# Attention feeding routed experts on one core: banks, places and order of the score maxima and of three small products

## The chip, the cores and the metric

One core of a Trainium2 chip runs one program. The metric is device time in microseconds of one execution; each kernel is given by the median of several runs. Engines: TensorE (PE; its weight loads PEld), VectorE (DVE), ScalarE (ACT), GpSimd (POOL), SyncE (SP, which issues DMAs). TensorE writes PSUM, which has eight banks of 512 fp32 columns for each of 128 partitions; VectorE and ScalarE read them.

## The reference

```
q_pool = q.reshape(8, 8, 576, 2, 64).mean(axis=3)        # 8 batches, 8 heads, 1152 keys
scores = q_pool @ k.T / 8
attn   = softmax(scores, axis=-1)                         # its maximum subtracted
x      = (attn @ v) as 4608 tokens x 512
logits = x @ w_gate + modality_bias[modality_id]          # 8 experts
e      = argmax(logits); g = softmax(logits)[e]
out    = g * (relu(x @ w1[e]) @ w2[e])                    # 512 -> 1024 -> 512
```

All inputs are fp32.

## The kernel before

**Tiles and stages.** Two batches of one head make a *pair*; there are 32 pairs. For each pair the kernel finds for every query a bound on its scores (the *row*: minus the maximum over all keys of the high fp16 part), computes the scores (L978, L979, fp16 with high and low parts, into one of three banks `psc`), takes the exponential on ScalarE (L980, 432 columns each), splits off the exponentials' low part `Pl` (L961 on ScalarE, L963 on VectorE) and multiplies with the values (L1038 to L1040) into bank X0 for the first head of the pair and X1 for the second. `evac` (L1056 to L1061) divides by the sums. The experts follow after all pairs.

**Order of the work.** Every engine's queue is written out by hand. The loop at the end of `attention` goes through 18 *steps* for each pair (`NSTEP`), and strings of letters (`ORD`) say what each step issues: `s` a score part, `v` the value products of 128 queries (three of them), `E` an event, `J` a piece of routing, `F` what was put off with `later`. `ends(t)` then issues what is due at the end of a step. Times such as `T_SQ = -19` count steps from the start of the pair that the work is for, so work for a pair is done during the two pairs ahead of it. Step numbers below are those within a pair, 0 to 17.

**Five shared banks.** Besides the three `psc` banks there are M0 and M1 (one tile `pm` of two banks), M2, X0 and X1. A product into a bank waits for whoever read it before.

- For pairs 0 to 2 `first_max` and `maxpass` compute score maxima block by block, through M0, M1 and M2 in turn.
- From pair 3 on, six *events* for each pair do this: block 4 (step 13), event 0 (16), event 1 (1), the rest (4), event 2 (7) and event 3 (10). Events 0 to 3 issue four products of 512 columns (L921): in the order M0, M2, M1, X0 or X1. VectorE takes the maxima (L903): M0 and M1 in one instruction of 1024 columns, then M2, then X0 or X1. After event 3 the maxima are combined (`m`, L843), and three steps later, at the end of step 13, TensorE transposes them into M2 (L847), VectorE makes the row `mr` (L856) and SP sends it to the score operand B2.
- Other products use `some()`, which is M2 while events run: the routing product (L289) in step 9 of every second pair, whose result VectorE adds to the logits (L295) in step 10; the scales' product (L787, `power`) at the end of step 2, read by `half` (L793) and two more small instructions (L795); the placing products of the router (L353, L355), allowed only in steps 2, 3, 13, 14 and 15.

**The scales.** `square` (step 17) sums the squares of a pair's values on ScalarE (L781), `power` and `scales` make powers of two of it, GpSimd copies one (`both`, L802) and scales the values (VH, L823, steps 3 and 4). GpSimd's first VH (`values` with part 1) and its sum of the queries (`split_q`, L688) wait for VectorE's latest L963 (`hold`).

```
ORD = ('NvJMvsvMsvXF', 'JvvsEMvvXFvv', 'vFvvsJvXv')
later_end(PD if p else 0, lambda: scales(p, pt))
```

Of the kernel before, what the change touches and what calls it, by code (L numbers as in the profile page):

```python
# [9 lines left out]
F32 = mybir.dt.float32  # L10
# [8 lines left out]
PSUM = bass.MemoryType.PSUM  # L19
# [3 lines left out]
P = 128  # L23
# [15 lines left out]
NSTEP = 2 * NKC  # L39
# [38 lines left out]
V1 = (9, 11, (14, 15), 18, (18, 19))  # L78
LOWS0 = (((0, 1152, 'A', 2), (1152, 1728, 'D', 3)),)
LAG0 = 7  # L80
T_SQ = -19
T_POW = -16
T_VH = (-14, -15)
T_VL = (-11, -2)
T_VS = -12
# [73 lines left out]
T_MX2 = -23  # L159
BY_HEADS = 3  # L160
EVENTS = (("block4", -23), (0, -20), (1, -17), ("rest", -14), (2, -11), (3, -8))
T_ROW = 3
M0, M1, X0, M2, X1 = range(5)
FIN = 0
FD = 0
# [446 lines left out]
def attention(tc, ctx, att, ident, npairs, xpool, on_two, on_split, on_scale, jobs, side, set_pm, started, ahead, hip):  # L612
# [7 lines left out]
    pvl = ctx.enter_context(tc.tile_pool(name="avl", bufs=3))  # L620
    sm = ctx.enter_context(tc.tile_pool(name="asm", bufs=3))
    ps_sc = ctx.enter_context(tc.tile_pool(name="pssc", bufs=3, space=PSUM))
    ps_all = ctx.enter_context(tc.tile_pool(name="psall", bufs=1, space=PSUM))
    m01 = ps_all.tile([P, 2, 512], F32, name="pm")
    m2, x0, x1 = (ps_all.tile([P, 512], F32, name=n) for n in ("pm2", "xp0", "xp1"))
    banks = [m01[:, 0], m01[:, 1], x0, m2, x1]
    turns3 = itertools.cycle((M0, M1, M2))
    now, flushed = [0], [-1]
    by_events = lambda: BY_HEADS * NSTEP + EVENTS[0][1] <= now[0] < (npairs - 1) * NSTEP
    bank = lambda: banks[next(turns3)]  # L630
    some = lambda: banks[M2] if by_events() else bank()
    set_pm(some, lambda: by_events() and now[0] % NSTEP not in (2, 3, 13, 14, 15))

    ones = const.tile([P, 1], BF16, name="ones")
# [204 lines left out]
    def row(p, mp, u0, u1):  # L839

        n = u1 - u0
        m9 = sm.tile([P, 9], F32, name="m9")
        nc.vector.tensor_reduce(m9[:, 0:n], mp[:, u0:u1], op=ALU.max, axis=AX.X, negate=True)  # L843

        def finish():
            pt = some() if p else banks[X1 if u0 else X0]
            nc.tensor.transpose(pt[0:n, 0:P], m9[:, 0:n], ident)  # L847
            if now[0] > NSTEP:
                later_end(FD, lambda: put(pt))
            else:  # L850
                put(pt)

        def put(pt):
            mr = sm.tile([9, P], F16, name="mr", bufs=1)
            made.add((p, f"row{u1}"))
            nc.vector.tensor_scalar(mr[0:n], pt[0:n, 0:P], 1.0 / ROW, 16.0 * math.log(PSC) / ROW, op0=ALU.mult, op1=ALU.add)  # L856
            done = st[p]["row"] = (nc.sync if p or u0 else nc.scalar).dma_start(out=B2[p % 2][D:D + 1, 2 * S + u0 * P:2 * S + u1 * P], in_=mr[0:n])
            if turns:
                with tc.issue_after(done.ins):
                    while turns:  # L860
                        turns.pop(0)()
        return finish
# [32 lines left out]
    def event(p, what):  # L895

        s = st[p]
        need(p, "qh", "hi0", "hi1")
        if "mp" not in s:
            s["mp"] = sm.tile([P, 9, 3], F32, name="mp")  # L900
        mp, hi = s["mp"], s["hi"]
        queries = lambda j, i: s["qh"][half[j], j * D + i * P:j * D + (i + 1) * P]
        most = lambda o, x: nc.vector.tensor_reduce(o, x, op=ALU.max, axis=AX.X)  # L903
        mixed = QB[p % 2][:, 4]
        if what == "block4":
            for t in range(2):
                nc.tensor.matmul(banks[M0 + t], mixed, hi[:, t * 512:(t + 1) * 512], start=True, stop=True)
            most(mp[:, 4, 0:2], m01)
        elif what == "rest":
            nc.tensor.matmul(banks[M1][:, 0:P], mixed, hi[:, 1024:S], start=True, stop=True, skip_group_check=True)  # L910
            for i in range(4):
                for j, b in ((0, M0), (1, M2)):
                    nc.tensor.matmul(banks[b][:, i * P:(i + 1) * P], queries(j, i), hi[half[j], 1024:S], start=True, stop=True, skip_group_check=True)
            by_block = lambda x: x.rearrange("p (u k) -> p u k", k=P)
            most(mp[:, 5:9, 2], by_block(m2))
            most(mp[:, 0:5, 2], by_block(m01.rearrange("p b n -> p (b n)")[:, 0:5 * P]))
        else:
            second = (M2, X0 if what < 2 else X1)
            for t in range(2):
                for j, to in ((0, M0 + t), (1, second[t])):  # L920
                    nc.tensor.matmul(banks[to], queries(j, what), hi[half[j], t * 512:(t + 1) * 512], start=True, stop=True)  # L921
            most(mp[:, what, 0:2], m01)
            for t in range(2):
                most(mp[:, 5 + what, t:t + 1], banks[second[t]])
        if what == EVENTS[-1][0]:
            later_end(T_ROW, row(p, mp, 0, 9))

# [147 lines left out]
    mxq, pvq, scq = [], [], []  # L1075
# [20 lines left out]
    def advance(q, n):  # L1096
        for _ in range(n):
            while q and next(q[0], DONE) is DONE:
                q.pop(0)
# [82 lines left out]
    for p in range(npairs):  # L1182
        b = NSTEP * p
# [54 lines left out]
    for t in range(NSTEP * npairs):  # L1238
        p, c18 = divmod(t, NSTEP)
        now[0] = t  # L1240
        if jobs and c18 in (JOBS if p < npairs - 1 else JOBS_LAST):
            running.append(jobs.pop(0))
        for a in ORD[t % len(ORD)]:
            if a == "J":
                running[:] = [g for g in running if next(g, DONE) is not DONE]
# [509 lines left out]
```

## Time and profile before

| | us |
|---|---|
| median of 3 runs (1200.7 to 1202.91) | 1201.41 |
| the profiled execution, its own time | 1202.61 |
| its span, first to last instruction | 1200.8 |
| TensorE busy | 1109.9 |
| VectorE busy | 982.9 |
| ScalarE busy | 893.7 |
| GpSimd busy | 438.0 |

The rows come from that one profiled execution. Times count from the start of its span. "Idle before" is the time that an engine stood ahead of an instruction, with the instruction that ended the wait behind the arrow. Instructions of an engine overlap a little at their ends, so the start of the next one can lie before the end of the last. PEclk is the granted share of TensorE's clock: 1.00 is 2.4 GHz, 0.50 is 1.2 GHz.

### The profile page before, as it was taken

What the parts mean: (1) busy time and instruction counts of PE and PEld (TensorE: products, weight loads), DVE (VectorE), ACT (ScalarE), POOL (GpSimd) and SP (SyncE); (2) the same over time, 40 slices, a digit from 0 to 9 for tenths busy, and PEclk for the clock granted to TensorE, in tenths of its full rate; (3) what the DMA queues carried; (4) which work ended last, traced back from release to release, by engine and by line L of the source; (5) the groups of instructions that cost most, each with busy time, mean ns of one, the idle gap of its engine ahead of it and who ended that gap; (6) DMA issues with size and microseconds to landing.
All of it is one profiled execution on the core that took longest, in us unless ns stands there. A gap on an engine that the chain in (4) does not pass through costs nothing.

```text
span 1200.8 us, 36624 instructions
## 1 busy us (share of the span) xinstructions
PE 1109.9 (92%) x15060; PEld 787.3 (66%) x15060; DVE 982.9 (82%) x1730; ACT 893.7 (74%) x1403; POOL 438.0 (36%) x469
## 2 busy tenths in 40 slices
PE   7888989989889899898999989999999999999997
PEld 3566666666656666665666766677667676766665
DVE  6778979989878898987989999987798767575665
ACT  5778878878868788886888888887665656565654
POOL 7644434453434435443334544312322221212111
PEclk9999989999989999998999999999999999999999
DMA  7757667776676767866668676559999999999993
GB/s 220 201 119 167 162 154 165 180 173 164 147 153 170 174 163 164 184 148 157 164 147 184 175 164 132 126 163 284 289 269 271 316 272 280 269 290 279 280 275 116
DMA packets 179696, 237.41 MB, mean 198 GB/s; under 512 B 96479, under 2 KB 127215, under 8 KB 179520
## 3 DMA queue, kind: packets, MB, share of 16 engines
q1 hardware_dynamic: 169254, 206.65, 65.2%
q0 software_dynamic: 10256, 28.33, 11.4%
q8 instruction: 120, 1.97, 0.7%
q14 instruction: 56, 0.46, 0.1%
q10 hardware_dynamic: 10, 0.00, 0.0%
HBM read 163.22 MB, written 18.99 MB: 152 GB/s over the span
## 4 chain that ended last, share of the span: by engine, by line
PE 63%; DVE 33%; issue 2%; DMA 1%; ACT 1%; SPq 0%; POOL 0%; POOLq 0%
DVE mp L903 18%; PE psc L979 7%; PE psc L978 6%; PE ph L1411 5%; PE ph L1410 5%; PE ph L1412 5%; PE po L1519 5%; PE po L1517 5%; PE po L1518 5%; DVE Pl L963 5%; PE xp L1038 4%; PE xp L1040 3%; PE xp L1039 3%; PE pm L921 3%; DVE x L1007 2%; DVE x L1061 2%
## 5 line engine op out<-in xcount | busy, mean ns | idle before, releaser
L980 ACT ACTIVATE Pe<-psc 128x432 int32<-128x432 f32 x768 | 384.6, 527 | 135.8 <-PE psc L979 119.0
L1038 PE MATMUL xp<-VH,Pe 128*128 128x65 f16 x2880 | 354.6, 196 | 0.0
L1038 PEld LDWEIGHTS <-Pe 128*128 128x128 f16 x2880 | 270.1, 98 | 128.6 <-issue 85.0
L1040 PE MATMUL xp<-VS,Pl 128*128 128x65 f16 x2880 | 351.6, 194 | 0.8 <-DVE Pl L963 0.8
L1039 PE MATMUL xp<-vl,Pe 128*128 128x64 f16 x2880 | 350.9, 193 | 0.0
L903 DVE TENSOR_REDUCE mp<-pm 128x2 f32<-128x1024 f32 (+3 forms) x319 | 287.8, 940 | 67.0 <-PE xp L921 39.1
L979 PE MATMUL psc<-B 65*128 65x432 f16 (+2 forms) x1152 | 310.8, 293 | 1.9 <-DMA B<-mr 1.9
L978 PE MATMUL psc<-B 128*128 128x432 f16 (+2 forms) x1152 | 310.8, 292 | 0.2 <-ACT Pe L980 0.2
L1039 PEld LDWEIGHTS <-Pe 128*128 128x128 f16 x2880 | 269.6, 99 | 46.4 <-issue 2.4
L1040 PEld LDWEIGHTS <-Pl 128*128 128x128 f16 x2880 | 267.9, 98 | 1.2 <-DVE Pl L963 1.2
L961 ACT ACTIVATE Pl<-Pe 128x1152 f16<-128x1152 uint16 x186 | 216.5, 1164 | 5.9
L1411 PE MATMUL ph<-xpart,w1h 128*128 128x256 f16 x544 | 148.3, 273 | 0.0
L1412 PE MATMUL ph<-xpart,w1l 128*128 128x256 f16 x544 | 148.3, 273 | 0.0
L1410 PE MATMUL ph<-xpart,w1h 128*128 128x256 f16 x544 | 148.3, 273 | 0.0
L963 DVE TENSOR_SCALAR Pl<-Pe 128x576 f16<-128x576 uint16 (+1 forms) x198 | 125.9, 637 | 4.5 <-ACT Pe L980 3.5
L978 PEld LDWEIGHTS <-B 128*128 128x128 f16 x1152 | 113.5, 99 | 10.6 <-issue 4.8
L688 POOL TENSOR_TENSOR rawq<-rawq 128x576 f32<-128x576 f32 x31 | 43.8, 1414 | 210.0 <-DVE Pl L963 210.0
L979 PEld LDWEIGHTS <-B 65*128 65x128 f16 x1152 | 114.8, 100 | 7.8 <-issue 0.5
L1416 DVE SCALAR_TENSOR_TENSOR hl<-ph,hh 128x512 f16<-128x512 f32 x72 | 49.7, 690 | 73.2 <-ACT hh L1415 68.3
L1517 PE MATMUL po<-w2h,hh 128*128 128x512 f16 x288 | 109.2, 379 | 0.0
L1518 PE MATMUL po<-w2l,hh 128*128 128x512 f16 x288 | 109.2, 379 | 0.0
L1519 PE MATMUL po<-w2h,hl 128*128 128x512 f16 x288 | 109.2, 379 | 0.0
(300 smaller groups left out, 1927.3 us busy)
## 6 DMA issues: line engine op xcount, KB each, us to landing
w2r<-in_w_dram SPq DMA_DIRECT2D x76, 512.0 KB
w1r<-in_w_dram SPq DMA_DIRECT2D x72, 512.0 KB
rawv<-in_att_dram SPq DMA_DIRECT2D x32, 576.0 KB
B<-hi SPq DMA_DIRECT2D x128, 144.0 KB
rawq<-in_att_dram SPq DMA_DIRECT2D x31, 576.0 KB
rawk<-in_att_dram SPq DMA_DIRECT2D x31, 576.0 KB
B<-qh SPq DMA_DIRECT2D x128, 72.0 KB
B<-lo SPq DMA_DIRECT2D x64, 144.0 KB
```

Of the source, the lines that this page charges most:

```text
L903: most = lambda o, x: nc.vector.tensor_reduce(o, x, op=ALU.max, axis=AX.X)
L961: nc.scalar.activation(low, rest, AF.Copy, scale=LOW)
L963: fast[0] = (nc.vector if eng == 'D' else nc.gpsimd).tensor_single_scalar(low, rest, LOW, op=ALU.mult)
L978: nc.tensor.matmul(o, b1[:, ks], b1[:, qs], start=True, stop=False, skip_group_check=True)
L979: nc.tensor.matmul(o, b2[:, ks], b2[:, qs], start=False, stop=True, skip_group_check=True)
L980: nc.scalar.activation(Pe[:, D + x0:D + x1], pt, AF.Exp, scale=1.0 / 16)
L1038: nc.tensor.matmul(out, Ph[:, qs], vh[:, c, j, 0:D + 1], start=c == 0 and g == 0, stop=False, skip_group_check=True)
L1039: nc.tensor.matmul(out[:, 0:D], Ph[:, qs], vl[:, c, j], start=False, stop=False, skip_group_check=True)
L1040: nc.tensor.matmul(out, Pl[:, qs], vs[:, c, j, 0:D + 1], start=False, stop=c == NKC - 1, skip_group_check=True)
L1410: nc.tensor.matmul(o, hi[:, c, fs], xh[:, :, c], start=c == 0, stop=False)
L1411: nc.tensor.matmul(o, hi[:, c, fs], xl[:, :, c], start=False, stop=False)
L1412: nc.tensor.matmul(o, lo[:, c, fs], xh[:, :, c], start=False, stop=c == 3)
```

## The change

It does five things. M0, M1 and M2 are three tiles of one bank each until step 13 of pair 1; `join_banks` then issues one more piece of the maxima that are due, closes their pool, and takes a tile of two banks for M0 and M1 and one for M2. In events 0 to 3 the maxima of M2 and of X0 or X1 come ahead of those of M0 and M1. The square goes from step 17 to step 16 and the scales' product from the end of step 2 to the end of step 0 (pairs 2 and later). The row's transposing product goes from the end of step 13 to the end of step 12 (`T_ROW`) and keeps M2. Products that `some()` serves in steps 13, 14 and 15 go to X0.

```
-T_SQ = -19
-T_POW = -16
+T_SQ = -20
+T_POW = -18
...
-T_ROW = 3
+T_ROW = 2
...
-    ps_all = ctx.enter_context(tc.tile_pool(name="psall", bufs=1, space=PSUM))
-    m01 = ps_all.tile([P, 2, 512], F32, name="pm")
-    m2, x0, x1 = (ps_all.tile([P, 512], F32, name=n) for n in ("pm2", "xp0", "xp1"))
-    banks = [m01[:, 0], m01[:, 1], x0, m2, x1]
+    ps_x = ctx.enter_context(tc.tile_pool(name="psx", bufs=1, space=PSUM))
+    banks = {X0: ps_x.tile([P, 512], F32, name="xp0"), X1: ps_x.tile([P, 512], F32, name="xp1")}
+    singles = ExitStack()
+    ps_one = singles.enter_context(tc.tile_pool(name="psone", bufs=1, space=PSUM))
+    for i in (M0, M1, M2):
+        banks[i] = ps_one.tile([P, 512], F32, name=f"pm{i}")
     turns3 = itertools.cycle((M0, M1, M2))
+
+    def join_banks():
+        advance(mxq, 1)
+        assert not mxq
+        singles.close()
+        ps_two = ctx.enter_context(tc.tile_pool(name="pstwo", bufs=1, space=PSUM))
+        two, banks[M2] = ps_two.tile([P, 2, 512], F32, name="pm01"), ps_two.tile([P, 512], F32, name="pm2")
+        banks["both"], banks[M0], banks[M1] = two, two[:, 0], two[:, 1]
...
-    some = lambda: banks[M2] if by_events() else bank()
+    some = lambda: banks[X0 if now[0] % NSTEP in (13, 14, 15) else M2] if by_events() else bank()
+    apart = lambda: banks[M2] if by_events() else bank()
...
-            pt = some() if p else banks[X1 if u0 else X0]
+            pt = apart() if p else banks[X1 if u0 else X0]
...
-            most(mp[:, what, 0:2], m01)
             for t in range(2):
                 most(mp[:, 5 + what, t:t + 1], banks[second[t]])
+            most(mp[:, what, 0:2], banks["both"])
...
+        if t == BY_HEADS * NSTEP + EVENTS[0][1]:
+            join_banks()
```

## Rows read from the trace of the kernel before

**Rows 1.** Busy time of each engine in two stages (us from the span's start): length, then busy us and number of instructions of PE, PEld, DVE, ACT and POOL, granted clock, DMA share, GB/s.

```profile
14.00:75.00 61.00, 48.94 (x633) 32.71 (x630) 46.12 (x92) 43.82 (x71) 39.25 (x67) 0.97 0.62 168
75.00:790.00 715.00, 648.35 (x11145) 471.91 (x11146) 633.36 (x1179) 592.13 (x982) 302.38 (x299) 0.97 0.69 161
```

**Rows 2.** Who waited for whom, TensorE alone, 75 to 790 us: us in total, times, longest us.

```profile
PE pm L289 <- DVE mp L903: 23.5, 14, 2.0
PE pm L787 <- DVE mp L903: 18.7, 28, 1.2
PE pm L921 <- DVE mr L856: 8.3, 12, 0.7
PE pm L353 <- DVE mr L856: 7.5, 2, 3.7
...
PE psc L979 <- DMA B<-mr: 1.9, 1, 1.9
```

**Rows 3.** Busy time in short stretches, columns as in rows 1; the granted clock is the third number from the end.

```profile
117.60:121.00 3.40, 3.40 (x34) 1.99 (x32) 1.41 (x4) 2.50 (x4) 3.06 (x3) 0.50 0.59 174
155.20:158.50 3.30, 3.30 (x40) 2.05 (x38) 1.09 (x1) 2.29 (x4) 0.46 (x1) 0.50 0.69 143
...
346.30:353.10 6.80, 6.33 (x63) 4.09 (x63) 1.28 (x6) 2.62 (x5) 0.32 (x1) 0.50 0.62 150
...
612.60:615.90 3.30, 3.30 (x31) 2.15 (x29) 1.49 (x4) 1.24 (x3) 2.04 (x2) 0.50 0.16 57
216.80:220.10 3.30, 3.30 (x61) 2.31 (x58) 2.54 (x5) 2.47 (x4) 2.25 (x2) 1.00 0.42 160
```

**Rows 4.** TensorE's instructions in order of time: the scales' product of four pairs (start us, length us, line, operation, output from inputs, shape, count, idle time before it and who ended it).

```profile
207.74 0.16 PE L787 MATMUL pm<-ss,ones 128*128 128x1 bf16 x1 [0.62 <-DVE mp L903]
...
254.68 0.16 PE L787 MATMUL pm<-ss,ones 128*128 128x1 bf16 x1 [0.62 <-DVE mp L903]
...
405.39 0.16 PE L787 MATMUL pm<-ss,ones 128*128 128x1 bf16 x1 [0.62 <-DVE mp L903]
...
453.89 0.16 PE L787 MATMUL pm<-ss,ones 128*128 128x1 bf16 x1 [0.62 <-DVE mp L903]
```

**Rows 5.** VectorE's instructions in order of time, 394.5 to 424.5 us, columns as in rows 4 (like neighbours are merged: "x2").

```profile
394.91 0.18 DVE L843 TENSOR_REDUCE m<-mp 128x9 f32<-128x27 f32 x1
...
402.83 0.45 DVE L963 TENSOR_SCALAR Pl<-Pe 128x576 f16<-128x576 uint16 x1
...
406.17 0.45 DVE L963 TENSOR_SCALAR Pl<-Pe 128x576 f16<-128x576 uint16 x1
407.67 1.43 DVE L903 TENSOR_REDUCE mp<-pm 128x4 f32<-128x512 f32 x2 [1.05 <-PE pm L913]
...
410.24 1.53 DVE L963 TENSOR_SCALAR Pl<-Pe 128x576 f16<-128x576 uint16 x1
...
412.15 1.82 DVE L903 TENSOR_REDUCE mp<-pm 128x2 f32<-128x1024 f32 x2
...
420.81 0.18 DVE L843 TENSOR_REDUCE m<-mp 128x9 f32<-128x27 f32 x1
...
422.00 1.22 DVE L903 TENSOR_REDUCE mp<-pm 128x2 f32<-128x1024 f32 x1
```

**Rows 6.** TensorE's instructions in order of time in the same stretch, columns as in rows 4: block 4 (L907), event 1 (L921), the routing product (L289), the next block 4.

```profile
394.60 0.59 PE L907 MATMUL pm<-hi,QB 128*128 128x512 f16 x2
...
402.87 0.60 PE L921 MATMUL pm<-hi,qh 64*128 64x512 f16 x3
...
414.02 0.60 PE L289 MATMUL pm<-wgs,xt 128*128 128x24 bf16 x18 [1.53 <-DVE mp L903]
...
421.11 0.60 PE L907 MATMUL pm<-hi,QB 128*128 128x512 f16 x2
```

**Rows 7.** Instructions of all engines in order of time, 217.9 to 218.6 us: the routing addition and the first products of event 3, in a period whose clock does not fall.

```profile
217.99 0.38 DVE L295 TENSOR_TENSOR lg<-pm,lg 128x216 f32<-128x216 f32 x1
...
218.49 0.39 PE L921 MATMUL pm<-hi,qh 64*128 64x512 f16 x2
```

**Rows 8.** ScalarE's instructions in order of time: the square of a pair's values and its sum.

```profile
426.76 1.16 ACT L781 ACTIVATE vl<-rawv 128x1152 f16<-128x1152 f32 x1
427.81 0.20 ACT L781 ACTIVATION_READ_ACCUMULATOR vl<-rawv 128x1 bf16 x1
```

**Rows 9.** SyncE's queue in order of time: the load of the values that rows 8 square.

```profile
411.98 0.53 SPq L677 DMA_DIRECT2D rawv<-in_att_dram  x1
```

**Rows 10.** GpSimd's instructions in order of time: the scaled values.

```profile
409.55 1.90 POOL L823 TENSOR_SCALAR VH<-rawv,sc 128x640 f16<-128x640 f32 x1
```

**Rows 11.** VectorE's instructions in order of time, 26 to 32.5 us: maxima of the first pairs, three at a time.

```profile
27.60 1.89 DVE L879 TENSOR_REDUCE mp<-pm 128x1 f32<-128x512 f32 x3 [0.47 <-PE pm L878]
29.95 1.89 DVE L879 TENSOR_REDUCE mp<-pm 128x1 f32<-128x512 f32 x3 [0.47 <-PE pm L878]
```

**Rows 12.** Who waited for whom, TensorE alone, 14 to 75 us: us in total, times, longest us.

```profile
PE pm L878 <- DVE mp L879: 7.2, 15, 1.2
PE pm L847 <- DVE mp L879: 1.9, 1, 1.9
```

**Rows 13.** Busy time in two stretches of the start, columns as in rows 1.

```profile
26.00:35.00 9.00, 5.36 (x45) 2.78 (x44) 7.10 (x11) 7.04 (x12) 8.63 (x7) 1.00 0.69 157
46.00:57.00 11.00, 8.59 (x113) 5.96 (x112) 8.16 (x19) 7.41 (x12) 6.69 (x7) 0.84 0.66 199
```

More of the change, by code (lines that the diff above doesn't have):

```diff
@@ L907, in event @@
                 nc.tensor.matmul(banks[M0 + t], mixed, hi[:, t * 512:(t + 1) * 512], start=True, stop=True)
-            most(mp[:, 4, 0:2], m01)
+            most(mp[:, 4, 0:2], banks["both"])
         elif what == "rest":
@@ L914, in event @@
             by_block = lambda x: x.rearrange("p (u k) -> p u k", k=P)
-            most(mp[:, 5:9, 2], by_block(m2))
-            most(mp[:, 0:5, 2], by_block(m01.rearrange("p b n -> p (b n)")[:, 0:5 * P]))
+            most(mp[:, 5:9, 2], by_block(banks[M2]))
+            most(mp[:, 0:5, 2], by_block(banks["both"].rearrange("p b n -> p (b n)")[:, 0:5 * P]))
         else:
```

## Prediction

> **What bounds the kernel now.** I first cut the span into stages. Up to 75 us the first two pairs start up; from 75 to 790 us pairs run in a steady pattern; after that come the experts, which the change doesn't touch [rows 1]. In the steady stretch TensorE is idle for 715 − 648 = 67 us and VectorE for 715 − 633 = 82 us, so both are nearly full and neither can run away from the other: whatever TensorE wins must leave VectorE 633 us. Next I read who ends TensorE's idle time [rows 2]. Nearly all of it is VectorE giving a bank back late: 23.5 us before the routing product (L289), 18.7 us before the scales' product (L787), 8.3 us where an event overwrites the bank of the row (L921 after mr), 7.5 us before two placing products (L353). The reader should see that each has a fixed length and place, once per pair or per two pairs.
>
> Then the clock. Behind long waits the granted clock falls to 0.50 (1.2 of 2.4 GHz) for a stretch [rows 3]: eight times behind L289 (first and last shown), twice behind L353 (the longer one shown), once behind a late DMA of the row, but not behind every L289 (216.8: still 1.00). The price shows without any model. From one scales' product to the second after it, two pairs take 46.94 us without a fall and 48.50 us with one [rows 4]: 1.56 us, so eight falls behind L289 cost 12.5 us besides the waits themselves.
>
> Last I read one period on VectorE and TensorE side by side [rows 5, 6].
>
> **The change part by part**, on the times of these rows, for a period of two pairs; 29 pairs have events, so there are 14.5 periods.
>
> *Maxima of the single bank first (event order).* The routing product waits for the single bank's maxima, which come second of two reductions in 1.82 us from 412.15 [rows 5]. A double bank's took 1.22 us of it, so put first they end 0.6 to 0.7 us behind 412.15 instead of at 413.97, and TensorE goes on 1.1 to 1.2 us sooner; the wait of 1.53 us shrinks to 0.4. But VectorE's sum doesn't shrink: the routing addition (L295) still comes after all three maxima. It reads the bank that event 3 writes next. In a period without a fall it ends at 218.37 and event 3 starts at 218.49 [rows 7]: 0.1 us to spare. TensorE 1.1 us earlier will stand there for about 1.0 us instead. So in itself this part moves a wait from L289 to event 3. What it gains on VectorE: the first reduction needs one product of the four, 0.2 us sooner where VectorE is waiting.
>
> *Scales' product two steps earlier.* Its waits, 0.62 us twice a period, go: its bank was reduced a whole event before. But VectorE's first reading (half) now stands in its queue behind the low parts (L963) that end at 403.28, and event 1 begins at 402.87 [rows 5, 6] and its second product writes that bank. half would end at 403.45; event 1 stands 0.6 us, in both pairs. Queued behind it are the score and value products of that step; behind half on VectorE, event 1's maxima. The square moves one step up on ScalarE, ahead of an exponential. It takes 1.16 + 0.20 us [rows 8]; that exponential then frees its bank later, for the score product just ahead of event 1, so this wait and the one for half fall on one another: I count 0.6 once. Its input isn't late: the load of rawv is issued 14.8 us ahead of such a square [rows 8, 9]. On GpSimd the copy of the scales moves ahead of the queries' sum, 0.28 us in idle time, free; without that cover it would cost 0.28 us of GpSimd's chain.
>
> That chain speaks against this part. Between 406.17 and 411.77 VectorE waits 1.05 us for the last blocks' products, then runs L963, which takes 1.53 us in place of 0.45 and ends 0.3 us behind GpSimd's VH (409.55 + 1.90 = 411.45) [rows 5, 10]. VH's start hangs on the L963 of 406.17. So TensorE coming 0.62 us earlier shortens VectorE's wait and lengthens that L963: I take the whole 5.6 us as pinned. If L963 were merely slow and moved with its start, 0.6 us a pair would be won; that is the second case below. The Trainium skill ("SBUF — State Buffer", section "SBUF: two separate sides") says that VectorE and GpSimd share one port pair under an exclusive lock, held for a whole instruction, and that the loser fully blocks. By that rule the 5.6 us stay, as summed here; by shared speed 15 us more would go. The two ends, 0.3 us apart, agree with the lock.
>
> *Row one step earlier.* The row's product comes about 0.6 us ahead of block 4's. On the old times its input (m) ends at 395.09 and 420.99, while block 4 starts at 394.60 and 421.11 [rows 5, 6]: TensorE would stand 1.1 and 0.5 us. VectorE's 0.2 us gain per event takes some off; I take 0.9 together, ends 0.5 and 1.6. Gained: mr is read before block 4's maxima, so event 0 no longer stands in every second pair (8.3 us in 12 times, 0.7 us each [rows 2]). On SP the row's DMA goes out some 2 us sooner and passes nothing that waits: the one late landing, 1.9 us, goes [rows 2], and its fall [rows 3], about 1.6 us.
>
> Sum of the steady period: gone 1.1 + 1.24 + 0.7 = 3.0; new 1.0 + 1.2 + 0.9 = 3.1. That is +0.1 us a period, +1.5 us in all; ends −0.5 and +0.5 a period, −7 to +7, from those of the row's part.
>
> *The falls.* The waits left are 0.4 to 1.1 us each. Falls behind L289 came behind single waits of 1.53 us and more; I take 11 of the 12.5 us as gained, ends 4 and 12.5.
>
> *Placing products in the free bank.* The two placing products that stand 3.7 us each [rows 2] wait for mr, which VectorE makes behind block 4's maxima and the output's evacuation. In bank X0 they wait for that evacuation instead, which stands directly ahead of mr. Ends 0 (as long as now) and −7.5 us (gone); nearer to 0: with mr out of the way 1 us less each, −2 us.
>
> *First pairs on three single banks.* Today two of the three are one tile: every product into one half waits for the maxima of the other half. In 27.60 to 32.3 VectorE makes three maxima, stands 0.47 us, makes three more [rows 11]. The waits sum to 7.2 us, and one row product waits 1.9 us more [rows 12]; its stretch at 46 to 57 us has clock 0.84 [rows 13], a fall, another 1.6 us by [rows 4]. All this is 10.7 us at most; VectorE, 46 of 61 us busy [rows 1], takes over in places: I take −6.5, ends −2 and −10. The new joining of two banks issues one step of work early and adds no instruction.
>
> Sum: +1.5 − 11 − 3.5 (late row and its fall) − 2 − 6.5 = −21.5 us. The profiled execution is 1202.6 us with span 1200.8; the median shown, 1201.4, lies 1.2 below it. From the median: 1180 us.
>
> **The rivals.** *VectorE wins too* (chance 0.15): if L963 isn't pinned, about 0.5 us a pair is had besides, 29 × 0.5 = 15 us: 1165. For it: VectorE idles 82 us. Against: the lengthened L963 [rows 5, 10].
>
> *The falls stay* (0.15): several short waits near each other, 0.4 at L289, 1.0 at event 3, 0.9 at the row, bring the clock down as one long one did. Then 11 us are not had: 1191. Against it: 26 to 35 us is full of waits of 0.2 to 0.8 us, TensorE busy 5.4 of 9.0, at clock 1.00 [rows 13]. The Trainium skill ("TensorE: Matmul & The Clock Gate", section "A second HAM failure mode: psum-queue depth-cycling") tells of a kernel whose cycling through banks left short idles frequent enough that the clock went up and down. By that rule this rival holds; that window disagrees.
>
> *The banks of the first pairs still wait* (0.08), because something else orders those products: 1180 + 6.5 = 1186.5.
>
> *Slower* (0.10): event 1 waiting for half. If VectorE lags 0.6 us more there than on these rows, event 1 stands 1.2 us in each of 29 pairs instead of 0.6, its maxima, L963 and VH shift with it (the pinned 5.6 us starts later), L289 then waits 1.5 us or more again and keeps its falls: 29 × 0.6 + 11 = 28 us over the forecast, 1208. It decides from where half ends over 1 us behind event 1's start. For it: VectorE is full just there; against: the single bank's early reduction lets event 0's part end no later.
>
> **How the numbers follow.** The forecast keeps 0.52: 1180, with a range of its own from 1171 to 1189. About 0.2% (2.4 us) is what can be told from no change. The cases two, three and four are all faster; with the forecast 0.90, of which I give 0.04 to ends of theirs within 0.2%: 0.86 faster, 0.04 the same, 0.10 slower. The range reaches to the second and third case with the ends of the start and of the falls: 1163 to 1195.
>
> **What would show it.** Right: no wait at L787, none of event 0 for mr; waits for m before the row's product; event 1 waiting for half or for an exponential; event 3 waiting for L295 about 1 us in every second pair; at most three stretches of clock 0.50 between 75 and 790 us; TensorE's waits on L878 below 2 us and pair 2 starting some 7 us sooner. Wrong: L289 still at 1.5 us, or VectorE busy above 95% of a much shorter steady stretch (second case), or falls in every period (third).

## The result and the profile after

The changed kernel takes 1181.88 us (median of 4 runs, 1179.25 to 1182.24), against 1202.0 before on the same chip: a ratio of 0.983, 95% interval 0.981 to 0.985. The profiled execution took 1182.24 us with a span of 1180.5; before it was 1202.61 and 1200.8. The clock granted over the whole span rose from 0.978 to 0.992 in the profiled executions, and from 0.981 to 0.995 in the mean of all executions of the two kernels.

Line numbers of `attention` are 10 to 14 higher after the change: the scales' product L787 is now L799, the row's product L847 is L859, `mr` L856 is L868, the maxima L903 are L915, block 4 L907 is L919, the events L921 are L933, L963 is L975, VH L823 is L835, the first pairs' products and maxima L878 and L879 are L890 and L891. The router's L289, L295 and L353 stay.

Where the 20.3 us of the span came from, by the first and the last block 4 (pairs 3 and 31; of the last one, its second product) and the last value product:

| stretch, us | before | after | difference |
|---|---|---|---|
| start to the first block 4 | 73.2 | 65.0 | −8.2 |
| to the last block 4 (steady part) | 689.2 | 676.1 | −13.1 |
| to the last value product | 48.9 | 49.6 | +0.7 |
| the rest | 389.6 | 389.8 | +0.3 |

Busy time by stretch, columns as in [rows 1] (the steady part ends 20 us earlier now); the last two stretches are the first one of [rows 13] and the only stretch of clock 0.50 between the two blocks 4:

```profile
14.00:75.00 61.00, 55.39 (x774) 37.83 (x773) 52.63 (x109) 50.87 (x84) 40.85 (x69) 0.99 0.68 186
75.00:770.00 695.00, 632.85 (x11023) 461.47 (x11022) 636.38 (x1166) 587.55 (x971) 300.78 (x299) 1.00 0.73 165
...
26.00:35.00 9.00, 8.12 (x87) 4.94 (x87) 8.10 (x15) 8.90 (x16) 8.75 (x7) 1.00 0.60 142
...
523.60:530.20 6.60, 6.01 (x59) 3.88 (x58) 1.49 (x5) 2.30 (x5) 0.00 (x0) 0.50 0.67 161
```

Clock 1.00 in the steady part, where it was 0.97, is the first thing to see. The second: TensorE was busy 8.1 of the 9 us from 26 us on, not 5.4.

Who waited for whom on TensorE, 75 to 790 us, as in [rows 2]:

```profile
PE pm L933 <- DVE mp L915: 13.3, 15, 1.4
PE pm L289 <- DVE mp L915: 11.9, 14, 1.2
PE pm L859 <- DVE m L855: 10.6, 15, 0.7
PE psc L991 <- DMA B<-mr: 7.4, 8, 1.4
PE pm L933 <- DVE lg L295: 6.8, 10, 0.7
PE xp L353 <- DVE x L1073: 5.3, 2, 2.6
PE pm L933 <- DVE lg L293: 2.7, 4, 0.7
```

The wait at L289 is halved (23.5 to 11.9 us), those at the scales' product and for `mr` are gone, and four waits stand in their place. Three were forecast: the event's for `lg`, the row's product for `m`, the placing products for the evacuation `x`. One was forecast to vanish and grew instead: the score product's for the row's DMA, eight times where there was one. And event 3 waits for event 2's maxima, 0.9 us in every second pair.

The same waits in one period, TensorE in order of time:

```profile
419.83 0.59 PE L933 MATMUL pm<-hi,qh 64*128 64x512 f16 x3 [0.83 <-DVE mp L915]
423.54 0.28 PE L859 MATMUL pm<-ident,m 128*9 128x128 f32 x1 [0.70 <-DVE m L855]
431.05 0.34 PE L991 MATMUL psc<-B 65*128 65x432 f16 x1 [1.21 <-DMA B<-mr]
...
442.02 0.60 PE L289 MATMUL pm<-wgs,xt 128*128 128x24 bf16 x18 [0.73 <-DVE mp L915]
445.20 0.39 PE L933 MATMUL pm<-hi,qh 64*128 64x512 f16 x2 [0.68 <-DVE lg L295]
```

### The profile page after: what moved, and what is told of

Same layout as the page of the kernel before. It is cut to its first block, busy times and chain, and to the rows that moved or that the text cites. A ratio compares the mean times of both kernels' runs of the same rounds, so it can differ in the third digit from the quotient of the medians.

```text
span 1180.5 us, 36614 instructions
## 1 busy us (share of the span) xinstructions
PE 1100.3 (93%) x15060; PEld 781.2 (66%) x15060; DVE 990.5 (84%) x1730; ACT 894.6 (76%) x1403; POOL 439.1 (37%) x469
## 4 chain that ended last, share of the span: by engine, by line
PE 47%; DVE 37%; DMA 5%; ACT 5%; issue 4%; POOL 2%; POOLq 0%; SPq 0%; DVEq 0%
DVE mp L915 17%; DVE Pl L975 6%; PE po L1531 4%; PE po L1533 4%; PE po L1532 4%; PE ph L1424 4%; PE ph L1426 4%; PE ph L1425 4%; PE psc L991 4%; PE psc L990 4%; DMA B<-mr 4%; PE xp L1050 2%; DVE vl L831 2%; DVE x L1073 2%; DVE x L1019 2%
## 5 line engine op out<-in xcount | busy, mean ns | idle before, releaser
L1050 PE MATMUL xp<-VH,Pe 128*128 128x65 f16 x2880 | 349.1, 194 | 0.0
L1052 PE MATMUL xp<-VS,Pl 128*128 128x65 f16 x2880 | 346.2, 193 | 0.8 <-DVE Pl L975 0.8
L1051 PE MATMUL xp<-vl,Pe 128*128 128x64 f16 x2880 | 345.6, 192 | 0.0
L1050 PEld LDWEIGHTS <-Pe 128*128 128x128 f16 x2880 | 267.0, 98 | 106.1 <-issue 61.1
L915 DVE TENSOR_REDUCE mp<-pm 128x2 f32<-128x1024 f32 (+3 forms) x319 | 297.1, 939 | 43.4 <-PE pm L933 25.8
L991 PE MATMUL psc<-B 65*128 65x432 f16 (+2 forms) x1152 | 304.4, 288 | 8.7 <-DMA B<-mr 8.6
L990 PE MATMUL psc<-B 128*128 128x432 f16 (+2 forms) x1152 | 305.0, 287 | 1.6 <-ACT Pe L992 0.5
L1051 PEld LDWEIGHTS <-Pe 128*128 128x128 f16 x2880 | 266.5, 98 | 44.7 <-issue 0.4
L1052 PEld LDWEIGHTS <-Pl 128*128 128x128 f16 x2880 | 265.0, 97 | 1.2 <-DVE Pl L975 1.2
L975 DVE TENSOR_SCALAR Pl<-Pe 128x576 f16<-128x576 uint16 (+1 forms) x198 | 132.9, 672 | 4.4 <-ACT Pe L992 3.4
L991 PEld LDWEIGHTS <-B 65*128 65x128 f16 x1152 | 113.1, 98 | 11.7 <-issue 1.3
L835 POOL TENSOR_SCALAR VH<-rawv,sc 128x512 f16<-128x512 f32 (+1 forms) x60 | 104.4, 1740 | 42.7 <-PE psc L991 29.1
L1430 DVE SCALAR_TENSOR_TENSOR hl<-ph,hh 128x512 f16<-128x512 f32 x72 | 49.6, 688 | 75.6 <-ACT hh L1429 75.5
```

The lines of the kernel that those rows point to most:

```text
L975: fast[0] = (nc.vector if eng == 'D' else nc.gpsimd).tensor_single_scalar(low, rest, LOW, op=ALU.mult)
L990: nc.tensor.matmul(o, b1[:, ks], b1[:, qs], start=True, stop=False, skip_group_check=True)
L991: nc.tensor.matmul(o, b2[:, ks], b2[:, qs], start=False, stop=True, skip_group_check=True)
L1050: nc.tensor.matmul(out, Ph[:, qs], vh[:, c, j, 0:D + 1], start=c == 0 and g == 0, stop=False, skip_group_check=True)
L1051: nc.tensor.matmul(out[:, 0:D], Ph[:, qs], vl[:, c, j], start=False, stop=False, skip_group_check=True)
L1052: nc.tensor.matmul(out, Pl[:, qs], vs[:, c, j, 0:D + 1], start=False, stop=c == NKC - 1, skip_group_check=True)
```

## The experiments

Twelve kernels were run. Each ratio is to runs of the kernel before on the same chip, whose medians were 1200.3 to 1204.1. *Clock* is the granted clock over the span, the mean of all executions of a kernel. The other columns come from each kernel's one profiled execution. *Start* is the first block 4, *steady* the time from there to the second product of the last one, *period* the median time from a block 4 to the second after it, over the periods without a stretch of clock 0.50 (their number in brackets; overlapping periods count, the first is left out), and *at 0.50* the time at that clock between the first and the last block 4.

Two columns need care. Periods without a fall are not all alike (46.9 to 48.4 us in the kernel before), and each kernel has them at other places of the sequence, so two medians can differ for that reason alone. Where it matters, the text gives the mean difference over the places at which both kernels are free of falls. And falls differ from one execution to the next: over its six executions e1_order's clock goes from 0.983 to 0.990, and the profiled one stands at 0.990.

| kernel | parts | ratio to before (95%) | median | start | steady | period | at 0.50 | clock |
|---|---|---|---|---|---|---|---|---|
| before | none | 1 | 1201 | 73.2 | 689.2 | 47.26 (9) | 41.0 | 0.981 |
| after | all | 0.983 (0.981–0.985) | 1181.9 | 65.0 | 676.1 | 47.71 (24) | 6.8 | 0.995 |
| e1_order | order alone | 0.989 (0.987–0.991) | 1186.7 | 72.4 | 672.5 | 46.72 (20) | 13.7 | 0.987 |
| e2_banks | banks alone | 0.990 (0.988–0.992) | 1189.3 | 62.3 | 687.3 | 47.21 (9) | 37.5 | 0.984 |
| e3_scales | scales alone | 1.005 (1.003–1.008) | 1206.5 | 73.4 | 691.2 | 47.03 (9) | 41.0 | 0.978 |
| e4_row | row alone | 0.996 (0.994–0.998) | 1194.6 | 71.8 | 682.9 | 47.70 (16) | 20.5 | 0.989 |
| b1_order_banks | order, banks | 0.977 (0.974–0.980) | 1173.6 | 62.5 | 669.5 | 46.86 (22) | 10.2 | 0.991 |
| a1_row3 | all but row | 0.980 (0.977–0.983) | 1178.3 | 63.5 | 673.8 | 47.24 (20) | 13.7 | 0.993 |
| a2_scales | all but scales | 0.978 (0.975–0.981) | 1176.2 | 61.3 | 675.3 | 46.70 (14) | 27.3 | 0.992 |
| a3_order | all but order | 0.997 (0.995–0.999) | 1196.3 | 63.4 | 688.3 | 48.02 (15) | 23.9 | 0.985 |
| a4_late_k | all; an edit without effect | 0.985 (0.982–0.987) | 1183.8 | 62.9 | 679.7 | 47.73 (22) | 10.2 | 0.994 |
| a6_k_behind | all, rawk behind the row | 0.980 (0.977–0.983) | 1176.3 | 63.4 | 672.2 | 47.05 (22) | 6.8 | 0.995 |
| c1_single_both_x | order (varied), banks | 0.977 (0.974–0.981) | 1174.3 | 60.4 | 675.0 | 46.95 (20) | 20.5 | 0.990 |
| c2_scales_k | all but scales, rawk behind | 0.975 (0.973–0.978) | 1173.6 | 61.2 | 672.6 | 46.70 (18) | 20.5 | 0.989 |

### One part alone on the kernel before

**e1_order**, the maxima of the single banks first:

```
-            most(mp[:, what, 0:2], m01)
             for t in range(2):
                 most(mp[:, 5 + what, t:t + 1], banks[second[t]])
+            most(mp[:, what, 0:2], m01)
```

> The kernel before with one part alone: in events 0 to 3 the maxima of M2 and of X0 or X1 ahead of those of M0 and M1. Theory (the falls of the clock hang on the one long wait at L289): the wait at L289 shrinks from 1.5 to 2.0 us to 0.4 to 1.1 us, at most one stretch of clock 0.50 is left in the steady part besides those at L353, about 1 us of waiting appears in front of event 3, and the time falls by 10 to 17 us against before (about 1188). Rival 1 (the falls need the other parts too, since several short waits together bring the clock down): L289 is shorter but five or more falls stay, and the time falls by less than 6 us. Rival 2 (the reordering only moves waits): within 3 us of before.

14.2 us faster by the medians, the steady part 16.7 us shorter. The theory holds, with its numbers: L289 waits 1.2 us on average, and 13.7 us stand at clock 0.50 in place of 41.0 (over all executions the clock rises less, from 0.981 to 0.987). What it did not say is that the wait at the scales' product [rows 2] goes too; no line of it is left, 75 to 790 us:

```profile
PE pm L921 <- DVE mp L903: 18.3, 15, 1.7
PE pm L289 <- DVE mp L903: 16.2, 14, 1.6
PE pm L921 <- DVE mr L856: 7.7, 12, 0.7
PE pm L353 <- DVE mr L856: 6.8, 2, 3.4
PE pm L921 <- DVE lg L295: 6.8, 10, 0.7
```

M2, the bank of the scales' product, is one of the banks that VectorE now empties first.

**e2_banks**, `join_banks` and the three single tiles alone:

> The kernel before with one part alone: three banks of their own for the first pairs, joined at step 13 of pair 1. Theory: block 4 of pair 3 comes 7 to 8.5 us sooner, the steady part is as long as before (within 2 us, eight falls behind L289), and the time falls by 7 to 8 us (about 1194). Rival (part of the 8 us at the start is due to other parts, such as the scales' product of pair 2, or is given back later): 2 to 5 us.

11.7 us faster, more than the theory had: the first block 4 comes 10.9 us sooner, the steady part is 1.9 us shorter with nearly as much time at 0.50 as before.

**e3_scales**:

```
-T_SQ = -19
-T_POW = -16
+T_SQ = -20
+T_POW = -18
```

> The kernel before with one part alone: the square one step earlier and the scales' product two steps earlier. Theory: the waits of 0.62 us in front of the scales' product go (18.7 us of TensorE's idle time in all), but VectorE's small readings stand in front of the maxima of event 1 and nothing else moves, so the wait comes back within the same period: the time stays within 4 us of before, and L289 still waits 1.5 us or more with its falls. Rival 1 (they are had): 10 to 18 us faster. Rival 2 (VectorE's chain gets longer by what was moved): 8 to 18 us slower.

5.6 us slower. L289 waits 27.7 us in all, not 23.5, and a new wait for `half` stands at event 1 nine times, 75 to 790 us:

```profile
PE pm L289 <- DVE mp L903: 27.7, 14, 2.3
...
PE pm L921 <- DVE half L793: 3.0, 9, 0.6
```

The mechanism of the theory is there (the waits of 18.7 us go, the time isn't had), the size lies between theory and second rival. Against the profiled execution of before it is 3.9 us (that one lies 1.7 above the median here), 2.0 of them in the steady part.

**e4_row**, `T_ROW = 2`:

> The kernel before with one part alone: the row's product one step earlier. Theory: event 0's waits for mr (8.3 us in all) go, the row's product waits for m instead (0.1 to 0.9 us), and the row's DMA on SP's queue now goes out directly behind the issue of the load of rawk (about 0.1 us, where it was 1.5 us or more), so that in several pairs the score product waits for it, 0.2 to 1.9 us each; together within 4 us of before. Rival (the row is worth its 8.3 us): 6 to 9 us faster, no waits for the row's DMA.

6.3 us faster. That is the rival's time, but not for its reason: the period without a fall is 0.44 us *longer* (17.8 us of waits for `m`), so the row's step loses by itself, yet only half as much time stands at clock 0.50. L289 waits exactly as before [rows 2], and the two placing products wait 0.6 us each in place of 3.7, 75 to 790 us:

```profile
PE pm L289 <- DVE mp L903: 23.5, 14, 2.0
PE pm L787 <- DVE mp L903: 19.0, 29, 1.2
PE pm L847 <- DVE m L843: 17.8, 28, 0.9
PE psc L979 <- DMA B<-mr: 2.7, 3, 1.1
...
PE pm L353 <- DVE mr L856: 1.2, 2, 0.6
```

So the length of the wait at L289 alone doesn't decide whether the clock falls.

### Parts undone in the changed kernel

**a3_order**, the changed kernel with the lines of e1_order put back:

> The changed kernel with the maxima of events 0 to 3 in the old order. Theory (the steady part's whole gain is the order of the maxima: with it alone the steady part was 16.7 us shorter, with everything 13.1): the wait at L289 is 1.5 to 2.3 us again, eight or more units of 3.41 us at clock 0.50 are back, and the time is 1193 to 1200. Rival (the row one step earlier keeps half of the falls away on its own, as it did alone, with L289 waiting as long as before): five or six such units, 1186 to 1192.

1196.3, as the theory says: without the order the ratio is 0.997 in place of 0.983. Its waits, 75 to 790 us:

```profile
PE pm L289 <- DVE mp L915: 28.0, 14, 2.3
PE pm L859 <- DVE m L855: 17.8, 26, 0.9
```

L289 is back at 2.0 us a time. At clock 0.50 there are 23.9 us, fewer than the theory's eight units (this profiled execution took 1192.9 us, 3.4 under the median): like e4_row, with the row early about half of before's.

**b1_order_banks** undoes scales, row and placing products:

```
-T_SQ = -20
-T_POW = -18
+T_SQ = -19
+T_POW = -16
...
-T_ROW = 2
+T_ROW = 3
...
-    some = lambda: banks[X0 if now[0] % NSTEP in (13, 14, 15) else M2] if by_events() else bank()
+    some = lambda: banks[M2] if by_events() else bank()
```

> The changed kernel with three of its five parts undone (scales' product, row and placing products as before), so: order of the maxima and the three single banks alone. Theory (alone these two parts took 13.4 and 11.6 us off, the scales' part alone added 6.5; the two act in different stages, so they add up): 1174 to 1179 us, 3 to 8 us under the changed kernel's 1182. Rival (the parts undone are what keeps the clock up when the rest is in): five or more stretches of clock 0.50 in the steady part, 1182 to 1190.

1173.6, 0.4 us under the theory's range. The rival is out: 10.2 us stand at clock 0.50, all at the two placing products. Two of the five parts alone beat all five by 8 us, so the other three together cost.

**a1_row3** (`T_ROW = 3`) and **a2_scales** (`T_SQ = -19`, `T_POW = -16`) undo two of the three one at a time. The placing products were not undone alone.

> The changed kernel with the row's product one step later again. Theory (the row's step is about even in waits: 8.3 us of event 0 for mr against 10.6 us of the row's product for m and 7.4 us of score products for the row's DMA, and VectorE takes up part of it): the waits for m and for the row's DMA go, the one for mr comes back, 1177 to 1182. Rival (as alone, the row's step gives 5 us by fewer falls): 1185 to 1189.

> The changed kernel with the square and the scales' product where they were before. Theory (alone this part added 6.5 us, some 2 of them in the steady part besides falls): 1176 to 1181, waits of 0.6 us or less in front of the scales' product back. Rival (with the maxima in the new order the waits in front of the scales' product would be longer, so the part pays here): 1184 to 1190.

3.6 and 5.7 us under the changed kernel: both times lie in the theories' ranges. But a1_row3's six runs (1176.2 to 1182.6) overlap with the changed kernel's four, so its gain is not shown by them. In a1_row3 two waits for the row's DMA are left between 75 and 790 us, 2.7 us, where the theory had none. In a2_scales the waits in front of the scales' product, which the theory had back, stay away. What comes back is the longer wait at L289, 75 to 790 us, where the changed kernel has at most 1.2:

```profile
PE pm L289 <- DVE mp L915: 16.6, 14, 1.6
```

With it come falls: 27.3 us stand at clock 0.50, 13.7 of them behind L289, in place of 6.8 in all. The period without a fall is shorter (46.70 us against 47.71; 0.59 in the mean over 15 places, part of it the row's DMA, waited for once and not eight times), so in the profiled executions the steady parts are nearly equal, 675.3 and 676.1, and the start differs by 3.7 us.

### The late row

In the changed kernel the score product at 431.05 waits for the row's DMA. SP's queue before (first fence) and after (second), start and length of each issue:

```profile
396.19 0.46 SPq L657 DMA_DIRECT2D B<-lo  x1
396.70 0.58 SPq L673 DMA_DIRECT2D rawk<-in_att_dram  x1
399.38 0.80 SPq L857 DMA_DIRECT2D B<-mr  x1
```

```profile
422.10 0.33 SPq L684 DMA_DIRECT2D rawq<-in_att_dram  x1
424.57 0.47 SPq L669 DMA_DIRECT2D B<-lo  x1
425.09 0.58 SPq L685 DMA_DIRECT2D rawk<-in_att_dram  x1
425.77 0.80 SPq L869 DMA_DIRECT2D B<-mr  x1
```

The order is the same. Before, the row came 2.1 us behind the 576 KB of `rawk`, because `mr` was late; now it goes out 0.1 us behind it, in 24 of the 26 pairs from 90 us on that have a `rawk` load. SP hardly holds it back: the issue starts 0.03 us behind the end of `mr` before (first line), and 0.03 to 0.05 us behind it now in all but three of the 26 pairs (0.4 to 1.1 us in those):

```profile
399.08 0.27 DVE L856 TENSOR_SCALAR mr<-pm 9x128 f16<-9x128 f32 x1
...
425.46 0.27 DVE L868 TENSOR_SCALAR mr<-pm 9x128 f16<-9x128 f32 x1
```

What is late is the transfer. In 13 pairs the row's nine packets of 256 bytes can be told apart in the trace: the last of them ends 1.5 us after the issue's start before the change and 3.0 us after it now (medians). In the other pairs SP issues two transposes of `x` directly behind the row, whose packets have the same size. All eight waits lie in these.

**a4_late_k** issued that load five steps later in the loop:

```
+T_K = -41
...
-            nc.sync.dma_start(out=k, in_=att[p, :, 0:S])
+            if p < 3:
+                load_k(p)
...
             go(T_K2 - b if p == 2 else T_KQ, load_kq, end=False)
+            if p > 2:
+                go(T_K, load_k, end=False)
```

> The changed kernel with the load of rawk five steps later, so that SP issues it behind the row's DMA and not 0.1 us ahead of it. Theory (the row lands late because it travels beside 576 KB issued just ahead of it): the row's DMA lands sooner, the 7.4 us of waits for it go, and the time falls by 3 to 7 us against the changed kernel (1175 to 1179). Rival 1 (the row lands late because it is issued late, the load has nothing to do with it): the waits stay as they are, 1180 to 1184. Rival 2 (the waits go, but VectorE, which has no time to spare, lets TensorE wait as much elsewhere): 1180 to 1184 without those waits.

Nothing changed, and the trace says why: `rawk` still stood 0.1 us ahead of the row. The loop's order is that of TensorE, VectorE, ScalarE and GpSimd; SP's is set by the framework that lowers the program, so the sentence on queues ahead of the prediction is too broad. Past the first pairs this kernel's instructions are in the same order as the changed kernel's on all engines, which makes it a second measurement of that one: 1183.8 against 1181.9.

**a6_k_behind** ties the load to the row in SP's queue:

```
+    def load_k_behind(p):
+        with tc.issue_after(st[p - 2]["row"].ins) if "row" in st[p - 2] else ExitStack():
+            load_k(p)
...
+            if p > 2:
+                go(T_K, load_k_behind, end=False)
```

> The changed kernel with the load of rawk held behind the row's DMA in SP's queue (in a4_late_k the five steps changed nothing: SP's order is not that of the program, and rawk still stood directly ahead of the row's DMA). Theory (the row lands late because it travels beside 576 KB issued 0.1 us ahead of it, and 0.7 us of it is the wait for that issue): the 7.4 us of waits for the row's DMA shrink to 2.5 or less; the two-pair period without a fall goes from 47.7 to 47.2 or 47.4, the time to 1175 to 1180. Rival 1 (VectorE takes it up): the waits go, the period stays at 47.7, 1180 to 1184. Rival 2 (the load has nothing to do with it): the waits stay as they are.

SP's queue at the same place of the period:

```profile
419.10 0.33 SPq L685 DMA_DIRECT2D rawq<-in_att_dram  x1
421.57 0.47 SPq L670 DMA_DIRECT2D B<-lo  x1
422.75 0.79 SPq L878 DMA_DIRECT2D B<-mr  x1
423.64 2.71 SPq L1043 DMA_TRANSPOSE xt<-x  x2
426.40 0.58 SPq L690 DMA_DIRECT2D rawk<-in_att_dram  x1
```

No wait for the row's DMA is left between 75 and 790 us (one of 0.5 us stands at 70), while the others are as in the changed kernel (L289 11.8 us, event 3 13.3, the row's product 10.6). The period falls from 47.71 to 47.05 us (by 0.37 in the mean over 23 places, which the 14 periods make some 5 us), the time to 1176.3: 5.6 us under the changed kernel, and its five runs (1175.3 to 1176.8) lie below all four of that one. The theory holds, but for the 0.7 us that it gave to the wait for the issue: SP issues the row as long after block 4 as in the changed kernel (0.7 and 1.6 us in the two kinds of pairs, medians). What changed is what travels beside it: where the nine packets can be told apart, they end 1.5 us after the issue, as before the change.

### Two attempts to go further

**c1_single_both_x** puts the maxima of M0 and M1 between those of M2 and of X0 or X1, in b1_order_banks:

```
-            for t in range(2):
-                most(mp[:, 5 + what, t:t + 1], banks[second[t]])
+            most(mp[:, 5 + what, 0:1], banks[second[0]])
             most(mp[:, what, 0:2], banks["both"])
+            most(mp[:, 5 + what, 1:2], banks[second[1]])
```

> The kernel with the order of the maxima and the three single banks alone (b1_order_banks, 1173.6), with the maxima of M0 and M1 between those of M2 and those of X0 or X1, so that the first product of the next event finds M0 free 0.6 us sooner. Theory (VectorE is without a gap where event 3 waits 1.2 us for M0, so an earlier TensorE only waits behind it later): 1171 to 1176. Rival 1 (event 3's wait halves and the time with it): 1165 to 1170. Rival 2 (X1's maxima come too late for the fourth product): 1177 or more.

**c2_scales_k** is a6_k_behind with `T_SQ = -19` and `T_POW = -16`:

> The changed kernel with the scales' part as before and rawk behind the row's DMA, so the two corrections that paid one by one (a2_scales 1176.2, a6_k_behind 1176.3, the changed kernel 1181.9). Theory (both shortened the same thing: without a fall a two-pair period of 46.70 and 47.05 us where order and banks alone have 46.86, which is what VectorE allows): they don't add up, 1172 to 1177. Rival (they add up): 1168 to 1171.

1174.3 and 1173.6, both the theory: the first cut the events' waits for maxima from 17.7 to 11.4 us without any gain, the second joined two gains of 5.7 and 5.6 us to one of 8.3. The three fastest, b1, c1 and c2, can't be told apart.

## Why the prediction came out, point by point

1180 was forecast, 1181.9 came. That the sum comes so close is in part luck, because terms that were too small on either side cancel: the falls and the start gave 3 to 4.5 and 1.7 us more than forecast, the period with the late row lost 4 to 7 us more.

**The steady part** (forecast about −15, measured −13.1) splits into three estimates. 28 block-4 gaps are 14 periods. (1) The period without a fall grew, by 0.28 us in the mean over the nine places that are free of falls in both kernels and by 0.45 by the medians: 14 times that is +4.0 to +6.3. (2) 41.0 us at clock 0.50 became 6.8. At the price of [rows 4], 1.56 us for a stretch of 3.4, that is −15.6; at half the length of each stretch it is −17.1. (3) The two long waits of L353 went from 7.5 to 5.3 us: −2.2. Together −13.8 by the first figures and −13.0 by the second.

- **The falls**: forecast −11 and −1.6, measured −15.6 to −17.1. All eight behind L289 are gone. The reason given, that they follow a single wait of 1.53 us and more, holds in so far as in none of the profiled executions a stretch of clock 0.50 stands behind a wait at L289 of less than 1.48 us. It is not enough: e4_row halved the falls with L289 unchanged. Nor is it the order of the maxima alone, as the prediction had it. In the five kernels with the new order and the scales' product in its old place (e1_order, b1_order_banks, a2_scales, c1_single_both_x, c2_scales_k) L289 still waits up to 1.6 us, in three of them stretches stand behind it, and the clock is 0.987 to 0.992. In the four with the order and the early scales' product (after, a1_row3, a4_late_k, a6_k_behind) it waits 1.2 us at most, no stretch stands behind it, and the clock is 0.993 to 0.995. The rival in which several short waits bring the clock down did not come about: 14 waits of 0.85 us at L289, 15 of 0.9 at event 3 and eight for the row came with 6.8 us at clock 0.50 in all, at a placing product that waited 2.6. The Trainium skill ("TensorE: Matmul & The Clock Gate", section "A second HAM failure mode: psum-queue depth-cycling") tells of a kernel in which frequent short idles between groups of products did bring it down; these waits did not.
- **The period**: forecast +1.5 in all, less 1.9 for the late landing, measured +4.0 to +6.3. Without the late row it would have come out: over the same nine places a6_k_behind's period is as long as before's (0.00 us). Inside the sum two terms were wrong and cancel: the order won 0.30 us a period by itself (e1_order, nine places) where 0.1 was booked, and the scales' part cost 0.25, below.
- **The placing products**: forecast −2, measured −2.2: they wait 2.6 us each for the evacuation, as described. But it is not bank X0 that won this. With the late row they wait 3.4 us each in M2 (b1_order_banks) and 3.2 in X0 (a1_row3). With the early row they wait 0.6 in M2 (e4_row) and 2.6 in X0: the early row had taken `mr` out of their way, and X0 put the evacuation there. The changed kernel with these products in M2 was not run, so what this part costs there stays open.

How a period goes, TensorE's start of each piece counted from a block 4, medians over the periods without a fall that begin with the pair that has the routing product (`e0` to `e3` events, `sc` the scales' product, `rt` the routing product; the first period is left out). The scales' part shows by c2_scales_k against a6_k_behind, the late row by a6_k_behind against after:

```
             b4   e0    e1    sc    rest   e2    rt    e3     b4     e0     e1     sc    rest    e2     e3     b4
before      0.0  3.75  8.29 10.80  12.49 15.92 19.52 21.63  25.03  28.51  32.00  34.52  36.20  39.64  43.12  47.11
e1_order    0.0  3.48  7.97  9.70  11.39 14.82 17.93 20.05  24.49  27.97  31.46  33.20  34.89  38.32  43.31  46.80
c2_scales_k 0.0  3.37  6.87  8.60  10.29 13.72 16.81 18.93  23.77  27.15  30.64  32.37  34.06  37.49  42.43  46.82
a6_k_behind 0.0  3.37  7.29  6.40  10.86 14.29 17.05 19.16  24.01  27.38  31.30  30.42  34.77  38.20  42.70  47.09
after       0.0  3.37  7.99  7.31  11.38 14.82 17.79 19.91  24.75  28.12  32.04  31.16  35.51  38.94  43.35  47.73
```

- **Order**: from event 1 to the scales' product 2.51 us before, 1.73 in e1_order, twice; from event 2 to the routing product 3.60, now 3.11. Taken back at event 3: 1.04 us between it and block 4 in the first half, 1.51 ahead of it in the second. The forecast had the first of these returns and not the second, and L289 kept 0.85 us, not 0.4.
- **Scales**: reckoned for the wrong waits. The 1.24 us a period booked for the waits at the scales' product were won by the order already, so with the new order its new place had none of them left to win. It costs instead: over the 19 places free of falls in both, a period is 0.25 us longer in a6_k_behind than in c2_scales_k. From event 0 to event 1 takes 3.92 us in the one and 3.50 in the other, in both halves: 0.42 of the 0.6 forecast, some 0.2 of it the moved product itself, and no wait for `half` or for an exponential is listed there. TensorE's shorter waits at L289 and event 3 give part of it back. The start pays as well, which no term had: the first block 4 comes at 62.9 to 65.0 us in the five kernels with the three banks and the early scales' product, and at 60.4 to 62.5 in the five with the banks and the old place. What the part wins, no term had either: the falls that stay away, above. By the medians it costs 5.7 us (a2_scales against after) or 2.7 (c2_scales_k against a6_k_behind); in the steady part of the profiled executions it is even (675.3 against 676.1, and 672.6 against 672.2).
- **The pinned stretch** holds. From the L963 (now L975) ahead of the last blocks' maxima to the end of the lengthened one VectorE took 5.60 us [rows 5, 10], and in the changed kernel 5.60 again, 411.38 to 416.98:

```profile
411.38 0.45 DVE L975 TENSOR_SCALAR Pl<-Pe 128x576 f16<-128x576 uint16 x1
412.60 1.42 DVE L915 TENSOR_REDUCE mp<-pm 128x4 f32<-128x512 f32 x2 [0.78 <-PE pm L925]
...
415.18 1.80 DVE L975 TENSOR_SCALAR Pl<-Pe 128x576 f16<-128x576 uint16 x1
```

```profile
414.77 1.89 POOL L835 TENSOR_SCALAR VH<-rawv,sc 128x640 f16<-128x640 f32 x1
```

  VectorE's wait for TensorE is 0.27 us shorter than the 1.05 of before, and the L975 beside VH is 0.27 us longer than the 1.53. It ends 0.3 us behind VH, as before. The stretch takes 5.6 to 5.7 us in 25 of 27 pairs before and in 26 of 28 after, and the second case, in which VectorE wins too, is out. That is the lock of the Trainium skill ("SBUF — State Buffer", section "SBUF: two separate sides"), and the trace agrees; the Trainium skill ties it there to certain forms of VectorE's instruction, and whether L975 has such a form the trace doesn't show.
- **Row**: the wait for `mr` in event 0 is gone and the one for `m` is there, 0.7 us, as forecast. The sentence that the row's DMA goes out sooner and passes nothing that waits is the step that failed: it goes out 2.5 to 3.2 us sooner after block 4, and that brought it next to `rawk`. Instead of −1.9 us in all this came to +0.37 us a period (a6_k_behind against after, 23 places), some 5 us; the steady parts differ by 3.9 and the medians by 5.6.

**The start**: forecast −6.5 with ends −2 and −10, measured −8.2, and −9.7 to −12.8 by the nine other kernels with the three banks (first block 4 at 60.4 to 63.5; the changed kernel's 65.0 is the latest). Waits and fall summed to 10.7; the 4.2 taken off because VectorE would take over were too much. Its maxima now run eight in a row where [rows 11] show three and a gap:

```profile
26.86 4.87 DVE L891 TENSOR_REDUCE mp<-pm 128x1 f32<-128x512 f32 x8 [1.48 <-PE pm L890]
```

The **slower** rival needed event 1 to stand 1.2 us in each pair and L289 to wait 1.5 again. It stood about 0.4, and L289's longest was 1.2.

## What to carry to other kernels

When several parts of a change shorten waits on the same bank, ask of each what it still wins once the others are in: here reordering two reductions freed the bank for the scales' product too, and the early row freed the placing products better in their old bank than in the new one. When something small is made ready earlier, read what stands directly ahead of it in its queue: the row was issued sooner and waited for more often, because its slack had been what kept it away from a 576 KB load. And time stretches with and without falls of the clock apart, at the same places of the sequence: the row's step and the scales' part both lost in the period and won in the falls.

## What the runs showed of the hardware

- With the same waits at L289 (23.5 us in 14 times, longest 2.0) the time at clock 0.50 was 41.0 us in the kernel before and 20.5 in e4_row. What else brings it down stays open.
- The nine 256-byte packets of a row DMA issued 0.1 us behind a load of 576 KB ended 3.0 us after the issue, and 1.5 us after it where the load was issued 1.5 us and more ahead (before) or behind (a6_k_behind); medians of 13 pairs each. Where transposes were issued behind such a row as well, a score product waited until 5.3 us after the issue (425.77 to 431.05); with the load behind the row none waited in the steady part.
- VectorE's instruction beside GpSimd's lengthened from 0.45 us to 1.53 before and 1.80 after at the place shown, and ended 0.3 us behind it in all 27 pairs before and all 28 after, whenever it started.
